# First product in three-chunk steps: a 128-row matmul per chunk and three 19-row matmuls on 32-row tiles

## The chip, the cores and the metric

The kernel runs on one core of one Trainium2 chip. The core has five engines with queues of their own: PE (TensorE, matmuls; its weight loads are shown as PEld), DVE (VectorE), ACT (ScalarE), POOL (GpSimd) and SP (SyncE, which here issues all the transfers). The metric is device time in microseconds, from launch to end, as the median of several runs.

## The reference

Four batches of 12480 tokens attend to 49 agents, which attend to the keys; the result goes through a feed-forward layer.

```python
def sm(a, b):
    s = scale * (a @ b.transpose(0, 2, 1))
    s = s - s.max(-1, keepdims=True)
    e = np.exp(s)
    return e / (e.sum(-1, keepdims=True) + 1e-09)
a2k = sm(agents, k)          # [4, 49, 12480]
agent_v = a2k @ v            # [4, 49, 128]
q2a = sm(q, agents)          # [4, 12480, 49]
x = q2a @ agent_v            # [4, 12480, 128], as 49920 rows
h = x @ w_in                 # w_in [128, 2048]
g = h - np.tanh(h)
out = g @ w_out              # w_out [2048, 128]
```

All inputs are float32; outputs are float32.

## The kernel before

**Folded product.** Since x = q2a @ agent_v, the kernel never forms x. Per batch it computes aw = agent_v @ w_in (49 x 2048) once, and h of a block is aw transposed times the 49 attention weights of each token. A block is 480 tokens (BLK), a batch has 26 blocks, and there are 104 of them. The 2048 hidden units are 16 chunks of 128 (NCH). Each chunk's h is a PSUM tile part of 128 units by 480 tokens.

**Two-part numbers.** A matmul in the fp32r format keeps only part of a float32's bits, so operands are split in a rounded high part and a low remainder. The attention weights lie in `pT` as 98 rows: 49 high parts and 49 low parts (pp, lines 376 and 378). `aw` lies in two tensors, `awh` and `awl`, each with 98 rows: both halves hold the same 49 rows (line 304), rounded for awh, the remainder for awl. `m1` (line 393) adds two matmuls per chunk: awh times pT (line 398) and awl times pT (line 399). The second product does the same with three matmuls: wo_l times gh, wo_h times gh, wo_h times gl (lines 459 to 461).

**One step** is a pair of chunks (n, i): block n, pair i of 8. Four m1 matmuls fill an h tile of two PSUM banks (three such tiles). ACT computes tanh of the scaled h into y (line 408) and its square into z (line 410). Since |h| is small in this data, h - tanh(h) is about h * z up to a constant factor; DVE forms g = h * z (line 412). POOL rounds g to gh (line 442), DVE computes gl = g - gh (line 447), and six m2 matmuls add to the block's output `acc` in a `misc` bank (two such banks, which the other small jobs also use). Where h is too large a general path is chosen at the end (line 588 on); it does not run with these inputs. In even blocks the last pair (PLAIN_PAIR, 7) is "plain": g goes unsplit into full-precision float32 matmuls with wo_f (line 457), four passes for two chunks, and lines 442 and 447 are left out.

**Order.** Program order staggers the work: step k issues m1 of step k, lines 408 to 442 of step k, line 447 of step k - 1 and m2 of step k - 2 (LAG1, LAG2). This order only sets priorities; the framework fixes each engine's queue at build time, with its own model of when an operand is ready, so that m1 of a later step may come between two m2 matmuls.

**Side jobs.** Generators run beside the steps, one part per step (`live`). Counted in positions 0 to 15 of a double block (two blocks): position 0 loads 960 query columns (`q_load`), 3 starts `q_softmax`, 13 starts `q_transpose` for the next even block and 2 for the odd one. `q_transpose` fills a misc bank with four transposes (line 385), and one position later ACT copies it to pT (line 390). At positions from KS the jobs of the next batch's `phase1` start: scores (line 228), the value products (line 276), and `project`, which makes aw in column parts (PCUT) by lines 327 to 331. For batch 0 all of this comes ahead of the loop, save the later parts of project. Key tiles use 3 buffers and value tiles 4 (KV, VB).

**Queues.** SP issues the loads of q, k and v and the store of each double block's output (line 524), in one line of order.

Of the kernel before, what the change touches and what calls it, by code (L numbers as in the profile page):

```python
# [24 lines left out]
A2 = 2 * A  # L25
FF = 2048
# [46 lines left out]
class Build:  # L73
    def __init__(self, ctx, tc, aps):
# [12 lines left out]
    def wtile(self, tag, bufs):  # L87
        return self.work.tile([128, 1024], F32, tag=tag, name=tag, bufs=bufs)
# [4 lines left out]
    def constants(self):  # L93
# [15 lines left out]
        self.wo_f = c.tile([128, 2, C], F32, tag="wo_f", name="wo_f")  # L109
        self.vb = [c.tile([128, GT, C + 2], F32, tag=f"v{i}", name=f"v{i}") for i in range(VB)]  # L110
        for vt in self.vb:
            nc.gpsimd.memset(vt[:, :, C : C + 1], 1.0)
# [38 lines left out]
    def load_w_out(self, c, raw):  # L151
# [7 lines left out]
        if c == PLAIN_PAIR // 2:  # L159
            nc.scalar.copy(self.wo_f.rearrange("p n e -> p (n e)"), w[:, 2 * C * (PLAIN_PAIR % 2) :][:, : 2 * C])  # L160

    def phase1(self, b):
        nc = self.nc
        st = {}
        kb, vb = (KV0 if b == 0 else KV), VB
# [7 lines left out]
        def load_k(g):  # L173
            n = tiles(g)
            kt = self.work.tile([128, GT * 128], F32, tag="kv", name="kt", bufs=kb)
            kt = kt.rearrange("p (t n) -> p t n", n=128)[:, :n, :]
            nc.sync.dma_start(kt, self.kT[b][:, g * GT : g * GT + n, :])
            return kt

        def load_v(g):  # L180
            vt = self.vb[g % VB]
# [13 lines left out]
        def scores(g):  # L195
# [7 lines left out]
            kt = ahead("k", load_k, g, kb if b == 0 else kb - 1)  # L203
            if b and g >= NG - vb:
                ahead("v", load_v, 0, g - NG + vb + 1)
            if b == 0:
                ps = self.ph.tile([128, 2, 512], F32, tag="h", name="h")
# [50 lines left out]
        def av(g):  # L258
            vt = ahead("v", load_v, g, vb - 1)
# [8 lines left out]
            if b == 0:  # L268
                if g == 0:
                    st["ps"] = self.ph.tile([128, 2, 512], F32, tag="h", name="h")[:, 0, :]  # L270
# [39 lines left out]
    def project(self, b, bound):  # L310
        nc = self.nc

        def part(c, lo, hi):
            yield
            yield
            if c == 0:
                self.aw[b] = tuple(
                    self.keep.tile([128, FF], F32R, tag=t, name=t, bufs=2) for t in ("awh", "awl")
                )
            awh, awl = self.aw[b]  # L320
# [8 lines left out]
            h = awh[:A2, sl]  # L329
            nc.scalar.copy(h, ps)  # L330
            nc.vector.tensor_tensor(awl[:A2, sl], ps, h.bitcast(F32), ALU.subtract)
            if bound:
                nc.vector.tensor_reduce(
                    self.mx[:A, NP * b + c : NP * b + c + 1],
                    awh[:A, sl].bitcast(F32),
# [45 lines left out]
    def q_transpose(self, pp, half, res):  # L381
# [7 lines left out]
        pT = self.keep.tile([128, BLK], F32R, tag="pT", name="pT", bufs=3)  # L389
        nc.scalar.copy(pT[:A2], ps[:A2, :BLK])  # L390
        res.append(pT)

    def m1(self, aw, pT, i):
        nc = self.nc
        h = self.ph.tile([128, 2, 512], F32, tag="h", name="h")
        for c in range(2):
            sl = slice((2 * i + c) * 128, (2 * i + c + 1) * 128)
            nc.tensor.matmul(h[:, c, :BLK], aw[0][:A2, sl], pT[:A2], start=True, stop=False)  # L398
            nc.tensor.matmul(h[:, c, :BLK], aw[1][:A2, sl], pT[:A2], start=False, stop=True)  # L399
        return h  # L400

    def pair(self, t):
        return t[:, : 2 * BLK].rearrange("p (c n) -> p c n", c=2)

    def act(self, h):
        nc = self.nc
        y = self.pair(self.wtile("y", NB["y"]))
        nc.scalar.activation(y, h[:, :, :BLK], AF.Tanh, scale=TSC)  # L408
        z = self.wtile("z", NB["z"])[:, : 2 * BLK]
        nc.scalar.activation(z, y.rearrange("p c n -> p (c n)"), AF.Square)  # L410
        g = self.wtile("g", NB["g"])[:, : 2 * BLK]
        nc.vector.tensor_tensor(self.pair(g), h[:, :, :BLK], self.pair(z), ALU.mult)  # L412
        return g

    def act_general(self, h):
        nc = self.nc
        hv = h[:, :, :BLK]
        d = self.wtile("y", NB["y"])[:, : 2 * BLK]
        u = self.wtile("z", NB["z"])[:, : 2 * BLK]
        nc.scalar.activation(self.pair(d), hv, AF.Tanh)  # L420
        nc.scalar.activation(self.pair(u), hv, AF.Square)
        nc.vector.tensor_tensor(self.pair(d), hv, self.pair(d), ALU.subtract)
        big = self.wtile("y", NB["y"])[:, : 2 * BLK]
        nc.vector.tensor_scalar(big, u, 4.0, None, ALU.is_ge)
        nc.vector.tensor_scalar(u, u, 16.0, None, ALU.min)
        r = self.wtile("z", NB["z"])[:, : 2 * BLK]
        nc.vector.tensor_scalar(r, u, 1.0 / 15.0, 13.0, ALU.mult, ALU.add)
        g = self.wtile("g", NB["g"])[:, : 2 * BLK]
# [7 lines left out]
        nc.vector.tensor_tensor(self.pair(g), hv, self.pair(g), ALU.mult)  # L436
# [3 lines left out]
    def high(self, g):  # L440
        gh = self.wtile("gh", NB["gh"])[:, : 2 * BLK].bitcast(F32R)
# [3 lines left out]
    def low(self, g, gh):  # L445
        gl = self.wtile("gl", NB["gl"])[:, : 2 * BLK].bitcast(F32R)
# [3 lines left out]
    def m2(self, acc, i, gh, gl):  # L450
        nc = self.nc
        for c in range(2):
            f = 2 * i + c
# [190 lines left out]
```

## Time and profile before

| what | value |
|---|---|
| runs, median (lowest to highest) | 2228.51 us (2228.47 to 2228.87), 3 runs |
| profiled execution, span from first to last instruction | 2226.8 us |
| granted TensorE clock, mean | 0.992 |
| PE busy | 2181.5 us, 98% |
| DVE busy | 2044.3 us, 92% |
| ACT busy | 1812.7 us, 81% |
| POOL busy | 1410.9 us, 63% |
| share of 16 DMA engines, loads and stores | 15.1% |

The span is the profiled execution's own time as far as the profile tells it; the median of the runs is 1.7 us longer and also holds what lies around the instructions. Busy times are unions: two matmuls that overlap count once. A row of a group reads: line, engine, operation, output <- inputs, shapes, count | busy us, mean ns of one | idle time of the engine before them and what ended it. A timeline row begins with start and duration in us. Matmul durations include the time until the last result is out, so consecutive matmuls overlap in the trace; what one costs is seen from start to start.

### The profile page before, as it was taken

How to read it: one execution, taken by the hardware profiler on the slowest of the kernel's cores; microseconds unless marked ns; L12 is line 12 of the kernel's file. 1: busy time of each engine (PE TensorE's matmuls, PEld its weight loads, DVE VectorE, ACT ScalarE, POOL GpSimd, SP SyncE). 2: the span in 40 equal slices, each digit the busy share in tenths (PEclk: the TensorE clock that was granted, in tenths of full speed). 3: DMA queues.
4: the chain of work that ended last, by engine and by line, in shares of the span. 5: the costliest groups of instructions: out<-in, count | busy, mean ns of one | idle time of the engine just before them, and what ended most of it. 6: DMA issues, size and time to landing. Idle time of an engine off the chain costs nothing.

```text
span 2226.8 us, 31246 instructions
## 1 busy us (share of the span) xinstructions
PE 2181.5 (98%) x11083; PEld 1838.3 (83%) x11083; DVE 2044.3 (92%) x2107; ACT 1812.7 (81%) x2179; POOL 1410.9 (63%) x957
## 2 busy tenths in 40 slices
PE   7699999999999999999999999999999999999998
PEld 7588878888888887888888888788888888888887
DVE  6998998889998999888999999988999999999998
ACT  3478887778887877877888878877889989898987
POOL 2555566656765647665666555766666767676776
PEclk9899999999999999999999999999999999999999
DMA  9411111211011110211011210121010000000000
GB/s 300 120 56 56 57 37 47 65 50 35 28 46 56 56 58 30 63 56 58 19 36 38 65 55 21 37 64 49 19 36 19 28 27 28 27 27 27 27 10 20
DMA packets 76658, 108.75 MB, mean 49 GB/s; under 512 B 4048, under 2 KB 56528, under 8 KB 76496
## 3 DMA queue, kind: packets, MB, share of 16 engines
q1 hardware_dynamic: 76496, 106.68, 15.1%
q8 instruction: 91, 1.49, 0.3%
q14 instruction: 71, 0.58, 0.1%
HBM read 81.10 MB, written 25.56 MB: 48 GB/s over the span
## 4 chain that ended last, share of the span: by engine, by line
PE 90%; DVE 5%; POOL 2%; issue 1%; ACT 1%; DMA 0%; POOLq 0%; SPq 0%; ACTq 0%; DVEq 0%
PE h L398 16%; PE h L399 15%; PE misc L461 15%; PE misc L459 14%; PE misc L460 14%; PE misc L457 4%; PE misc L353 4%; PE misc L276 3%; PE misc L228 3%; DVE gl L447 1%; DVE g L412 1%; POOL gh L442 1%; PE h L209 1%; PE misc L385 1%; PE misc L327 0%
## 5 line engine op out<-in xcount | busy, mean ns | idle before, releaser
L442 POOL TENSOR_SCALAR gh<-g 128x960 fp32r<-128x960 f32 x780 | 1201.8, 1542 | 636.1 <-DVE g L412 488.9
L447 DVE TENSOR_TENSOR gl<-g,gh 128x960 fp32r<-128x960 f32 x780 | 977.6, 1254 | 88.6 <-PE misc L461 62.3
L412 DVE TENSOR_TENSOR g<-h,z 128x960 f32<-128x960 f32 x832 | 950.9, 1147 | 55.7 <-ACT z L410 53.3
L408 ACT ACTIVATE y<-h 128x960 f32<-128x960 f32 x832 | 804.2, 971 | 214.1 <-PE h L399 207.6
L410 ACT ACTIVATE z<-y 128x960 f32<-128x960 f32 x832 | 832.5, 1007 | 24.8 <-DVE g L412 7.8
L398 PE MATMUL h<-pT,awh 98*128 98x480 f32 x1664 | 666.9, 401 | 1.8 <-DVE g L412 1.3
L399 PE MATMUL h<-pT,awl 98*128 98x480 f32 x1664 | 631.6, 380 | 0.0
L461 PE MATMUL misc<-gl,wo_h 128*128 128x480 f32 x1560 | 608.7, 390 | 3.9 <-DVE gl L447 3.8
L459 PE MATMUL misc<-gh,wo_l 128*128 128x480 f32 x1560 | 594.2, 381 | 3.8 <-POOL gh L442 3.6
L460 PE MATMUL misc<-gh,wo_h 128*128 128x480 f32 x1560 | 591.2, 379 | 0.0
L398 PEld LDWEIGHTS h<-pT,awh 98*128 98x128 f32 x1664 | 312.8, 188 | 65.3 <-issue 14.0
L399 PEld LDWEIGHTS h<-pT,awl 98*128 98x128 f32 x1664 | 314.5, 189 | 58.8 <-issue 11.9
L461 PEld LDWEIGHTS misc<-gl,wo_h 128*128 128x128 f32 x1560 | 292.4, 187 | 59.1 <-DVE gl L447 8.7
L459 PEld LDWEIGHTS misc<-gh,wo_l 128*128 128x128 f32 x1560 | 294.3, 189 | 54.0 <-POOL gh L442 11.1
L460 PEld LDWEIGHTS misc<-gh,wo_h 128*128 128x128 f32 x1560 | 292.9, 188 | 47.9 <-issue 0.2
L378 POOL TENSOR_TENSOR pp<-qe,pp 120x392 fp32r<-120x392 f32 x52 | 70.6, 1357 | 67.9 <-ACT pp L376 67.6
L353 PEld LDWEIGHTS misc<-ag,qt 128*120 128x120 f32 x832 | 96.8, 187 | 3.3
L353 PE MATMUL misc<-ag,qt 128*120 128x49 f32 x832 | 94.2, 267 | 0.0
L457 PE MATMUL misc<-g,wo_f 128*128 128x480 f32 x208 | 92.6, 567 | 0.0
L366 POOL TENSOR_TENSOR qe<-qe,qm 120x392 f32<-120x392 f32 x52 | 71.0, 1366 | 30.0 <-ACT qe L364 29.9
L522 ACT ACTIVATE o<-misc 128x480 f32<-128x480 f32 x104 | 58.7, 565 | 36.4 <-PE misc L457 22.8
L276 PEld LDWEIGHTS misc<-v,ke 128*49 128x49 f32 (+1 forms) x588 | 62.0, 123 | 17.5 <-issue 12.9
(85 smaller groups left out, 993.7 us busy)
## 6 DMA issues: line engine op xcount, KB each, us to landing
qt<-qT SPq DMA_DIRECT2D x52, 480.0 KB, 3.4
outT<-o SPq DMA_DIRECT2D x52, 480.0 KB, 2.6
kt<-kT SPq DMA_DIRECT2D x48, 512.0 KB, 3.6
v<-v SPq DMA_DIRECT2D x48, 512.0 KB, 4.1
raw<-w_in SPq DMA_DIRECT2D x4, 512.0 KB, 7.8
raw<-w_out SPq DMA_DIRECT2D x4, 512.0 KB, 9.5
kt<-kT SPq DMA_DIRECT2D x4, 128.0 KB, 2.0
v<-v SPq DMA_DIRECT2D x4, 64.0 KB, 1.9
```

Of the source, the lines that this page charges most:

```text
L353: nc.tensor.matmul(ps[:TT, t * A : (t + 1) * A], qt[:, t * TT : (t + 1) * TT], self.ag[:, b, :], start=True, stop=True)
L398: nc.tensor.matmul(h[:, c, :BLK], aw[0][:A2, sl], pT[:A2], start=True, stop=False)
L399: nc.tensor.matmul(h[:, c, :BLK], aw[1][:A2, sl], pT[:A2], start=False, stop=True)
L408: nc.scalar.activation(y, h[:, :, :BLK], AF.Tanh, scale=TSC)
L410: nc.scalar.activation(z, y.rearrange("p c n -> p (c n)"), AF.Square)
L412: nc.vector.tensor_tensor(self.pair(g), h[:, :, :BLK], self.pair(z), ALU.mult)
L442: self.nc.gpsimd.tensor_scalar(gh, g, 1.0, 0.0, ALU.mult, ALU.add)
L447: self.nc.vector.tensor_tensor(gl, g, gh.bitcast(F32), ALU.subtract)
L457: nc.tensor.matmul(acc[:, :BLK], self.wo_f[:, c, :], gh[:, x], start=first, stop=last)
L459: nc.tensor.matmul(acc[:, :BLK], self.wo_l[:, f, :], gh[:, x], start=first, stop=False)
L460: nc.tensor.matmul(acc[:, :BLK], self.wo_h[:, f, :], gh[:, x], start=False, stop=False)
L461: nc.tensor.matmul(acc[:, :BLK], self.wo_h[:, f, :], gl[:, x], start=False, stop=last)
```

## The change

- awh and awl become `awx` and `awt`. awx has 128 rows: the 98 rows of awh, and below them 30 rows (AX1) of the low parts. The other 19 low rows (AX2) go to `awt`, four copies of the row range at partitions 0, 32, 64 and 96, chunk f at 32 * (f mod 4). Only the 49 low rows that meet the high parts of the attention weights are kept; the product of the two low parts, which awl times pT held before, is left out.
- pT grows to 128 rows: rows 98 to 127 repeat its first 30. A new tile `pR` holds rows 30 to 48 at each of the four 32-row offsets. Both are filled by transfers from pT on SP, five per block, after the copy of line 390. project issues such transfers for awx and awt, up to five per column part.
- m1 works on three consecutive chunks, which may belong to two blocks: three 128-row matmuls, then three 19-row matmuls, one on each of three 32-row tiles, which add to the same three banks. The h tile has three banks, and there are two of them.
- The elementwise work of lines 408, 410, 412, 442 and 447 covers 1440 columns per instruction instead of 960; the square is written to g and multiplied in place, so z goes.
- All chunks take the split path; the plain pairs and wo_f go.
- The side jobs keep their positions; a step of three chunks advances them once for each even chunk in it, so once or twice.
- Key tiles of batches 1 to 3 and value tiles share one ring of five buffers.

```diff
+AX1 = 128 - A2
+AX2 = A - AX1
+QR = 4
...
-PCUT = (0, 256, 768, 1280, 1792, 2048)
+PCUT = (0, 384, 768, 1280, 1792, 2048)
 NP = 5
 KV0 = 13
-KV = 3
-VB = 4
-PLAIN_PAIR = NCH // 2 - 1
-PLAIN_EVERY = 2
+RB = 5
+HP = NCH // 2
+W = 3
 LAG1 = 1
 LAG2 = 1
-NB = dict(y=2, z=2, g=4, gh=3, gl=2)
+NB = dict(y=2, g=3, gh=4, gl=2)
...
-        self.ph = ctx.enter_context(self.pool("ph", 3, space=PSUM))
+        self.ph = ctx.enter_context(self.pool("ph", 2, space=PSUM))
...
+    def slot(self):
+        self.nslot += 1
+        return self.kvb[self.nslot % RB]
...
+            if b == 0:
+                kt = self.work.tile([128, GT * 128], F32, tag="kv", name="kt", bufs=KV0)
+                kt = kt.rearrange("p (t n) -> p t n", n=128)[:, :n, :]
+            else:
+                kt = self.slot()[:, :n, :C]
...
+                awx = self.keep.tile([128, FF], F32R, tag="awx", name="awx", bufs=2)
+                awl = self.keep.tile([128, FF], F32R, tag="awl", name="awl", bufs=1)
+                awt = self.keep.tile([128, NCH // QR, 128], F32R, tag="awt", name="awt", bufs=2)
+                self.aw[b] = awx, awt, awl
+            awx, awt, awl = self.aw[b]
             sl = slice(lo, hi)
             if b == 0 and bound:
-                ps = self.ph.tile([128, 2, 512], F32, tag="h", name="h")[:, 0, :]
+                ps = self.htile()[:, 0, :]
             else:
                 ps = self.misc()
             ps = ps[:A2, : hi - lo]
             nc.tensor.matmul(ps, self.avs[:, b, :], self.w_in[:, sl], start=True, stop=True)
             yield
-            h = awh[:A2, sl]
+            h = awx[:A2, sl]
             nc.scalar.copy(h, ps)
-            nc.vector.tensor_tensor(awl[:A2, sl], ps, h.bitcast(F32), ALU.subtract)
+            nc.vector.tensor_tensor(awl[:A, sl], ps[:A], awx[:A, sl].bitcast(F32), ALU.subtract)
+            nc.sync.dma_start(awx[A2:, sl].bitcast(F32), awl[:AX1, sl].bitcast(F32))
+            lows = awl[AX1:A].bitcast(F32).rearrange("p (k q n) -> p q k n", q=QR, n=128)
+            for q in range(QR):
+                k0, k1 = -(-(lo // 128 - q) // QR), -(-(hi // 128 - q) // QR)
+                if k0 < k1:
+                    nc.sync.dma_start(awt[32 * q : 32 * q + AX2, k0:k1, :].bitcast(F32), lows[:, q, k0:k1, :])
...
         pT = self.keep.tile([128, BLK], F32R, tag="pT", name="pT", bufs=3)
+        pR = self.keep.tile([128, BLK], F32R, tag="pR", name="pR", bufs=3)
         nc.scalar.copy(pT[:A2], ps[:A2, :BLK])
-        res.append(pT)
-
-    def m1(self, aw, pT, i):
-        nc = self.nc
-        h = self.ph.tile([128, 2, 512], F32, tag="h", name="h")
-        for c in range(2):
-            sl = slice((2 * i + c) * 128, (2 * i + c + 1) * 128)
-            nc.tensor.matmul(h[:, c, :BLK], aw[0][:A2, sl], pT[:A2], start=True, stop=False)
-            nc.tensor.matmul(h[:, c, :BLK], aw[1][:A2, sl], pT[:A2], start=False, stop=True)
...
+        nc.sync.dma_start(pT[A2:].bitcast(F32), pT[:AX1].bitcast(F32))
+        for q in range(QR):
+            nc.sync.dma_start(pR[32 * q : 32 * q + AX2].bitcast(F32), pT[AX1:A].bitcast(F32))
+        res.append((pT, pR))
+
+    def m1(self, items, pT):
+        nc = self.nc
+        h = self.htile()
+        for c, (n, f) in enumerate(items):
+            awx = self.aw[n // NBLK][0]
+            nc.tensor.matmul(
+                h[:, c, :BLK], awx[:, f * 128 : (f + 1) * 128], pT[n][0][0], start=True, stop=False
+            )
+        for c, (n, f) in enumerate(items):
+            awt = self.aw[n // NBLK][1]
+            rows = slice(32 * (f % QR), 32 * (f % QR) + AX2)
+            nc.tensor.matmul(h[:, c, :BLK], awt[rows, f // QR, :], pT[n][0][1][rows], start=False, stop=True)
+        return h[:, : len(items), :BLK]
...
         nc = self.nc
-        y = self.pair(self.wtile("y", NB["y"]))
-        nc.scalar.activation(y, h[:, :, :BLK], AF.Tanh, scale=TSC)
-        z = self.wtile("z", NB["z"])[:, : 2 * BLK]
-        nc.scalar.activation(z, y.rearrange("p c n -> p (c n)"), AF.Square)
-        g = self.wtile("g", NB["g"])[:, : 2 * BLK]
-        nc.vector.tensor_tensor(self.pair(g), h[:, :, :BLK], self.pair(z), ALU.mult)
+        w = h.shape[1]
+        y = self.split(self.wtile("y", w))
+        g = self.wtile("g", w)
+        gv = self.split(g)
+        nc.scalar.activation(y, h, AF.Tanh, scale=TSC)
+        nc.scalar.activation(gv, y, AF.Square)
+        nc.vector.tensor_tensor(gv, h, gv, ALU.mult)
...
+    def m2(self, acc, f, c, gh, gl):
+        nc = self.nc
+        sl = slice(c * BLK, (c + 1) * BLK)
+        nc.tensor.matmul(acc[:, :BLK], self.wo_l[:, f, :], gh[:, sl], start=f == 0, stop=False)
+        nc.tensor.matmul(acc[:, :BLK], self.wo_h[:, f, :], gh[:, sl], start=False, stop=False)
+        nc.tensor.matmul(acc[:, :BLK], self.wo_h[:, f, :], gl[:, sl], start=False, stop=f == NCH - 1)
...
+                its, g, gh = q1.pop(0)
+                q2.append((its, gh, self.low(g, gh)))
 
         def out(keep):
             while len(q2) > keep:
-                n, i, gh, gl = q2.pop(0)
-                if i == 0:
-                    acc[n] = self.misc()
-                self.m2(acc[n], i, gh, gl)
-                if i == HP - 1:
-                    done.append(n)
-
-        for n, i in steps:
-            b = blocks[n][0]
-            pos = (n % 2) * HP + i
-            p = n // 2
-            if n % NBLK == 0 and i == 0 and b + 1 < B:
-                kq = self.phase1(b + 1)
-            h = foreground(n, i)
-            if n == 0 and i < len(rest0):
-                run(rest0[i])
+                its, gh, gl = q2.pop(0)
+                for c, (n, f) in enumerate(its):
+                    if f == 0:
+                        acc[n] = self.misc()
+                    self.m2(acc[n], f, c, gh, gl)
+                    if f == NCH - 1:
+                        done.append(n)
...
+        def begin(n, i):
+            p = n // 2
+            pos = (n % 2) * HP + i
...
+        for at in range(0, len(items), W):
+            its = items[at : at + W]
+            h = self.m1(its, pT)
+            while done:
+                finish(done.pop(0))
+            steps = [(n, f // 2) for n, f in its if f % 2 == 0]
+            for n, i in steps:
+                b = n // NBLK
+                if n % NBLK == 0 and i == 0 and b + 1 < B:
+                    kq = self.phase1(b + 1)
+                if n == 0 and i < len(rest0):
+                    run(rest0[i])
+                advance()
+                if n != steps[-1][0] or i != steps[-1][1]:
+                    begin(n, i)
+            g = self.act(h)
+            q1.append((its, g, self.high(g)))
+            low(LAG1)
+            out(LAG2)
+            if steps:
+                begin(*steps[-1])
```

More of the change, by code (lines that the diff above doesn't have):

```diff
@@ L108, in constants @@
         self.wo_l = c.tile([128, NCH, C], F32R, tag="wo_l", name="wo_l")
-        self.wo_f = c.tile([128, 2, C], F32, tag="wo_f", name="wo_f")
-        self.vb = [c.tile([128, GT, C + 2], F32, tag=f"v{i}", name=f"v{i}") for i in range(VB)]
-        for vt in self.vb:
+        self.kvb = [c.tile([128, GT, C + 2], F32, tag=f"v{i}", name=f"v{i}") for i in range(RB)]
+        for vt in self.kvb:
             nc.gpsimd.memset(vt[:, :, C : C + 1], 1.0)
```

99 lines of the change are left out of this document (32 added, 67 removed).

## The prediction

> **What bounds the kernel now.** I read the engine shares first, then two long windows (before and after 1850 us, where the score and value work for batches 1 to 3 ends), then the groups of instructions, then the timeline of single steps.
>
> ```profile
> PE 2181.5 (98%) x11083; PEld 1838.3 (83%) x11083; DVE 2044.3 (92%) x2107; ACT 1812.7 (81%) x2179; POOL 1410.9 (63%) x957
> PE 90%; DVE 5%; POOL 2%; issue 1%; ACT 1%; DMA 0%; POOLq 0%; SPq 0%; ACTq 0%; DVEq 0%
> 100.00:1850.00 1750.00, 1743.44 (x8844) 1465.99 (x8843) 1614.57 (x1642) 1450.76 (x1734) 1107.82 (x754) 1.00 0.14 44
> 1850.00:2200.00 350.00, 350.00 (x1692) 296.01 (x1691) 337.69 (x336) 314.83 (x363) 251.63 (x158) 1.00 0.07 25
> L412 DVE TENSOR_TENSOR g<-h,z 128x960 f32<-128x960 f32 x832 | 950.9, 1147 | 55.7 <-ACT z L410 53.3
> 100.00:1850.00 1750.00, 767.47 (x672) 1.00 0.14 44
> L412 DVE TENSOR_TENSOR g<-h,z 128x960 f32<-128x960 f32 x150 | 171.9, 1146 | 1.3 <-ACT z L410 0.5
> ```
>
> The first two rows give each engine's busy time and the chain that ended last; in the window rows the busy times of PE, PEld, DVE, ACT and POOL follow the length, then the granted clock, 1.00. PE is without a gap after 1850 and 99.6% busy before; DVE comes next with 337.69 of 350. The last row counts 150 pairs (one L412 each) in those 350 us. With 16 pairs to a double block (two 480-token blocks) that is 9.4 double blocks of 37.3 us. The first window holds 672 (the row above it, L412's DVE time and count alone): 42 double blocks of 41.7 us. DVE's share is 1614.57/42 = 38.4 us and, later, 36.0 us. So PE sets the pace, and DVE stands 1.3 us (late) to 3.3 us (early) per double block behind it: all that faster PE could win.
>
> ```profile
> 1994.46 1.14 DVE L412 TENSOR_TENSOR g<-h,z 128x960 f32<-128x960 f32 x1
> 1994.50 0.38 PE L398 MATMUL h<-pT,awh 98*128 98x480 f32 x1
> 1995.53 1.14 DVE L447 TENSOR_TENSOR gl<-g,gh 128x960 fp32r<-128x960 f32 x1
> 1996.60 1.14 DVE L412 TENSOR_TENSOR g<-h,z 128x960 f32<-128x960 f32 x1
> 1996.68 0.38 PE L398 MATMUL h<-pT,awh 98*128 98x480 f32 x1
> ```
>
> A matmul shows 0.38 us, but the ten of a pair start within 1996.68 - 1994.50 = 2.18 us: 0.218 us each is the price I use. DVE's two operations take 1.07 us each from start to start.
>
> **The change part by part.** Per chunk there were two 98-row matmuls. Now three chunks have three 128-row matmuls and three 19-row ones on 32-row tiles: 555 groups of three (1664/3).
>
> 1. The tile section. It replaces 3 x 0.218 = 0.654 us of PE. The trace has no 32-row tiles, but it has excursions to other tile shapes and back.
>
> ```profile
> 868.97 0.37 PE L399 MATMUL h<-pT,awl 98*128 98x480 f32 x1
> 869.27 1.49 PEld L276 LDWEIGHTS misc<-v,ke 128*49 128x49 f32 x14 [0.33 <-issue]
> 870.95 0.19 PEld L461 LDWEIGHTS misc<-gl,wo_h 128*128 128x128 f32 x1 [0.19 <-issue]
> 871.05 0.19 PEld L459 LDWEIGHTS misc<-gh,wo_l 128*128 128x128 f32 x1
> 842.80 0.38 PE L399 MATMUL h<-pT,awl 98*128 98x480 f32 x1
> 843.11 0.29 PEld L253 LDWEIGHTS misc<-dg,ones 49*128 49x128 f32 x2 [0.34 <-ACT z L410]
> 843.46 0.19 PEld L459 LDWEIGHTS misc<-gh,wo_l 128*128 128x128 f32 x1
> 843.57 0.19 PEld L460 LDWEIGHTS misc<-gh,wo_h 128*128 128x128 f32 x1
> L353 PEld LDWEIGHTS misc<-ag,qt 128*120 128x120 f32 x832 | 96.8, 187 | 3.3
> ```
>
> Before 49-column (L276) or 49-row (L253) weights the loader idles 0.33 us, and again 0.19 us after them; L353's full-height, 120-column weights do this nowhere (3.3 us over 832). So a change of tile shape empties the array. Worked out: the next matmul would start at 868.97 + 0.218 = 869.19, the load starts at 869.27, 0.08 late. Fourteen loads take 1.49 us, the last one 0.12 of it, so 0.105 us apart; they end their turn at 870.74. The next load comes 0.21 later, of which 129 columns stream 129/480 x 0.218 = 0.06, leaving 0.15 for the array to empty. The first full matmul streams 0.10 later, when the next load begins (871.05). L253 agrees: two loads of 128 columns 0.10 apart, 843.57 - 843.02 = 0.55 us in all.
>
> The new section is then 0.08 + 0.105 (first load) + 2d + 0.218 (480 columns) + 0.15 + 0.10 = 0.65 us + 2d, where d is the distance between neighbouring tiles. With d = 0 it costs what it replaces. Bounds: d = 0 from below, and 0.218 from above (one after the other). Below even that lies no emptying at all, 0.22 us. I take d = 0.105, L253's pace, the nearest row with 128-column weights on fewer than 128 rows: +0.21 us x 555 = +116 us; half that distance, 0.05, would give +55; bounds 0 and +241; without emptying -241.
>
> The Trainium skill, "TensorE: Matmul & The Clock Gate", Part 3, states that tiles in different row groups start about 4 ns apart; no run here shows it yet. By that rule d = 0.004 and this term would be about +4 us instead of +116.
>
> 2. No plain pairs. 52 pairs lose four full-precision passes each and gain six matmuls.
>
> ```profile
> 2202.55 1.77 PE L457 MATMUL misc<-g,wo_f 128*128 128x480 f32 x4
> L447 DVE TENSOR_TENSOR gl<-g,gh 128x960 fp32r<-128x960 f32 x780 | 977.6, 1254 | 88.6 <-PE misc L461 62.3
> L442 POOL TENSOR_SCALAR gh<-g 128x960 fp32r<-128x960 f32 x780 | 1201.8, 1542 | 636.1 <-DVE g L412 488.9
> ```
>
> PE: 6 x 0.218 - 1.77 = -0.46 us, x 52 = -24 us. DVE and POOL gain one L447 and one L442 per double block.
>
> 3. Three chunks per elementwise instruction.
>
> ```profile
> L522 ACT ACTIVATE o<-misc 128x480 f32<-128x480 f32 x104 | 58.7, 565 | 36.4 <-PE misc L457 22.8
> L408 ACT ACTIVATE y<-h 128x960 f32<-128x960 f32 x832 | 804.2, 971 | 214.1 <-PE h L399 207.6
> L410 ACT ACTIVATE z<-y 128x960 f32<-128x960 f32 x832 | 832.5, 1007 | 24.8 <-DVE g L412 7.8
> L363 DVE TENSOR_REDUCE qm<-misc 120x8 f32<-120x392 f32 x52 | 29.0, 559 | 3.2 <-PE misc L353 1.7
> ```
>
> DVE's slope is (1147 - 559)/568 = 1.035 ns per column, so 480 more cost 0.50 us: 1.57 per operation from start to start. Per double block 10.67 x 2 x 1.57 = 33.5 us, against 31 x 1.07 = 33.2 now: merging pays for the plain pairs, and DVE stays near 36 to 38 us. ACT's slope is (971 - 565)/480, or 0.41 us per chunk: tanh 1.38, square 1.42. Nothing on the path while PE leads. With PE at 41.7 - 0.5 + 10.67 x 0.21 = 43.4 us early and 39.1 late, DVE's 38.4 and 36.0 stay below.
>
> The h tiles are now two of three banks (six before and after). One is held for 0.65 + 0.86 + 1.38 + 1.42 + 1.64 = 5.95 us; two steps are at least 2 x 39.1/10.67 = 7.3 us. I cost this at nothing; if the 1.3 us of slack goes to the score work between, 1% (22 us). The other buffers (z gone, g three, gh four, one ring of five for k and v) I cost at nothing too, behind a DMA share of 0.14.
>
> 4. New transfers on SP: per block one that fills rows 98 to 127 of pT and four that fill pR, behind the ACT copy.
>
> ```profile
> 2000.25 0.34 SPq L524 DMA_DIRECT2D outT<-o  x1
> 2002.04 0.54 ACT L390 CAST pT<-misc 98x480 fp32r<-98x480 f32 x1
> 2002.60 0.98 ACT L408 ACTIVATE y<-h 128x960 f32<-128x960 f32 x1
> v<-v SPq DMA_DIRECT2D x4, 64.0 KB, 1.9
> v<-v SPq DMA_DIRECT2D x4, 32.0 KB, 2.8
> SPq L524 <- ACT o L522: 1168.8, 52, 37.3
> ```
>
> An issue takes about 0.34 us, a small landing 1.9 to 2.8 us; five in a row end 1.7 + 2.8 = 4.5 us after the copy at worst. The copy (L390) ends just as a step's tanh starts. For odd blocks it comes some five pairs ahead, and m2 work covers it. For even blocks (position 14) it comes in the step before its first use in two cases of three: a step is 39.1/10.67 = 3.66 us, its m1 1.51 of it, so 2.1 us ahead of the full matmuls late, 2.6 early. The first transfer takes 0.34 + 1.9 to 2.8, so they wait up to 1.0 us. Behind them on PE stand the m2 matmuls of the two groups before, and gh and gl come free later; the order is fixed at build time and may put those first. 35 blocks x 0.3 = +10 us, bounds 0 and 35 x 2.8 = 98. What shares SP's queue behind these (qt, kt, v, outT) has long waits already, as L524's row shows, with nobody late for it.
>
> 5. Start. The first tile needs awl's rows sent down the partitions before it can run, one issue and landing (2.2 to 3.1 us), once or twice; phase 1 of batch 0 has two h tiles instead of three. +5 us, bounds 0 to 10.
>
> Sum, against the profiled span: 2226.8 + 116 - 24 + 10 + 5 = 2333.8 us. The runs' median (2228.5) lies 1.7 above that span: 2335 us.
>
> **The rivals.**
>
> A. Tiles one after another (the change doesn't do what it says). d = 0.218: 2335 + 125 = 2460 us. For it: nowhere in this trace do two matmuls overlap by more than their tails. Against: other row groups use other rows and other PSUM banks.
>
> B. No emptying: the tile loads go ahead under the running full matmuls, and the section costs one matmul. It decides from a section under 0.65 us. PE's sum falls by 241 + 24 and DVE takes over at 38.4 early and 36.0 late. At its present late share (337.69/350 = 0.965) that makes 39.8 us early, 1.9 less than now, x 42 = -80 us; late nothing. 2228.5 - 80 + 5 = 2154 us, and no loss at block heads, as DVE has work. Against: the idle loader before L253, weights that also leave rows free.
>
> C. Emptying as above but tiles together, d near 0.004: 2335 - 112 = 2223 us, within the noise or just faster. This is the page's rule, worked out here from L276's rows. Against: no pair of loads of 128 columns stands closer than 0.10 us in these rows.
>
> D. The block heads: SP's five issues land late by a whole landing in 35 blocks: 2335 + 88 = 2423 us. For: the copy comes only one step ahead. Against: m2 matmuls of two earlier groups can fill.
>
> **How the numbers follow.** Forecast 0.47 (d between 0.05 and 0.12, 2270 to 2360), A 0.15, B 0.15, C 0.12, D 0.11. The range runs from C's lower side to A, 2205 to 2465, and leaves out B, 0.15. A measurement of this kernel tells about 0.2% from no change. Faster: B and half of C, 0.21. Same: a third of C, 0.04. Slower: the rest, 0.75.
>
> **What would show it.** Step 1: loader idle before each group's first 19-row load (0.3 us) and after its last (0.2 us), full-matmul starts 0.86 us plus 0.218 apart across the section; 0.65 says C, 1.09 says A, 0.22 says B. Step 2: no L457 and DVE below 95% busy. Step 3: DVE operations near 1.64 us. Step 4: at the first group of even blocks PE idle on a DMA, up to 1.0 us. I am wrong if DVE becomes the busiest engine or PE shows idle time above 2% of the loop.

## The result and the profile after

The changed kernel takes 2522.91 us (median of 4 runs, 2520.28 to 2526.86) against 2228.49 us (4 runs, 2228.28 to 2228.87) for the kernel before on the same chip: a ratio of 1.132, 95% interval 1.1304 to 1.1336. It is slower, as forecast, but by 294 us where 107 were expected, and outside the range. The profiled execution has a span of 2525.1 us and a mean granted clock of 0.952 (0.992 before).

From the page of the changed kernel: busy time of each engine, shares of the chain that ended last, and the costliest groups.

```profile
PE 2290.3 (91%) x11187; PEld 1670.2 (66%) x11187; DVE 2080.0 (82%) x1605; ACT 1733.8 (69%) x1624; POOL 1288.5 (51%) x733
...
PE 31%; DVE 22%; POOL 15%; issue 11%; ACT 11%; DMA 7%; SPq 2%; POOLq 0%; ACTq 0%; DVEq 0%
...
L464 POOL TENSOR_SCALAR gh<-g 128x1440 fp32r<-128x1440 f32 x555 | 1093.7, 1971 | 1040.1 <-DVE g L438 941.8
L469 DVE TENSOR_TENSOR gl<-g,gh 128x1440 fp32r<-128x1440 f32 x555 | 984.6, 1776 | 273.6 <-POOL gh L464 266.4
L436 ACT ACTIVATE y<-h 128x1440 f32<-128x1440 f32 x555 | 759.1, 1368 | 498.9 <-PE h L424 497.6
L438 DVE TENSOR_TENSOR g<-h,g 128x1440 f32<-128x1440 f32 x555 | 907.6, 1648 | 121.6 <-ACT g L437 120.1
```

Windows of the changed kernel over the same two stretches as before (length, then busy time and count of PE, PEld, DVE, ACT, POOL, then clock, DMA share, GB/s), and the second one again for line 438 on DVE alone, which counts the steps:

```profile
100.00:1850.00 1750.00, 1623.85 (x8058) 1186.32 (x8059) 1456.31 (x1106) 1235.60 (x1148) 910.45 (x510) 0.97 0.17 51
1850.00:2200.00 350.00, 314.33 (x1423) 222.20 (x1421) 292.56 (x208) 248.14 (x221) 179.26 (x98) 0.94 0.09 31
...
1850.00:2200.00 350.00, 132.65 (x82) 0.94 0.09 31
```

No engine is busy all the time any more. PE's share of the chain fell from 90% to 31%; DVE, POOL and ACT, issue time (11%) and DMA (7%) took the rest. The four engines wait in a ring: POOL waits 941.8 us for DVE's g, DVE waits 266.4 us for POOL's gh, ACT waits 497.6 us for PE's h, and PE waits for what DVE frees. PE stands idle 126.15 us (7%) early and 35.67 us (10%) late, where it had 0.4% and none. The late window holds 82 steps, 350/82 = 4.27 us each; the forecast was 39.1/10.67 = 3.66, the longer tile section included. So the loss shows as idle PE, with a lower granted clock besides (0.97 and 0.94 in the two windows, 1.00 before).

The tile section itself, in the changed kernel's timeline (start, duration), with two rows of the m2 matmuls that follow it, and the start of the loop:

```profile
91.52 1.54 PE L418 MATMUL h<-pT,awx 128*128 128x480 f32 x3 [0.37 <-ACT pp L392]
...
2202.70 0.19 PEld L424 LDWEIGHTS h<-pR,awt 19*128 19x128 f32 x3 [0.34 <-issue]
2202.70 0.49 PE L424 MATMUL h<-pR,awt 19*128 19x480 f32 x3
...
2301.21 0.81 PE L418 MATMUL h<-pT,awx 128*128 128x480 f32 x3
...
2302.36 0.49 PE L477 MATMUL misc<-gl,wo_h 128*128 128x480 f32 x1
2302.69 0.38 PE L475 MATMUL misc<-gh,wo_l 128*128 128x480 f32 x1
```

The loader idles 0.34 us ahead of the first 19-row load, as forecast. But the three loads take 0.19 us together, and the three matmuls 0.49 us together, where three full ones (L418) take 0.81: the tiles do run side by side. The section lasts from the end of the third full matmul's turn, 2301.21 + 3 x 0.217 = 2301.86, to the next full matmul's turn. That one (L477) ends its turn where L475 starts, so its turn begins at 2302.69 - 0.22 = 2302.47: 0.61 us, where 0.654 were replaced. By itself the section is 555 x 0.04 = 24 us cheaper than the matmuls it replaced, an estimate from this one section.

### The profile page after: what moved, and what is told of

It reads as the page before. It is cut to its first block, busy times and chain, and to the rows that moved or that the text cites. A ratio compares the mean times of both kernels' runs of the same rounds, so it can differ in the third digit from the quotient of the medians.

```text
span 2525.1 us, 30180 instructions
## 1 busy us (share of the span) xinstructions
PE 2290.3 (91%) x11187; PEld 1670.2 (66%) x11187; DVE 2080.0 (82%) x1605; ACT 1733.8 (69%) x1624; POOL 1288.5 (51%) x733
## 4 chain that ended last, share of the span: by engine, by line
PE 31%; DVE 22%; POOL 15%; issue 11%; ACT 11%; DMA 7%; SPq 2%; POOLq 0%; ACTq 0%; DVEq 0%
POOL gh L464 14%; DVE g L438 11%; PE misc L477 7%; DVE gl L469 6%; DMA pR<-pT 6%; PE misc L475 6%; PE misc L476 5%; ACT y L436 5%; ACT g L437 5%; PE h L418 4%; PE h L424 3%; PE misc L369 2%; PE misc L285 1%; SPq L410 1%; PE h L218 1%
## 5 line engine op out<-in xcount | busy, mean ns | idle before, releaser
L464 POOL TENSOR_SCALAR gh<-g 128x1440 fp32r<-128x1440 f32 x555 | 1093.7, 1971 | 1040.1 <-DVE g L438 941.8
L469 DVE TENSOR_TENSOR gl<-g,gh 128x1440 fp32r<-128x1440 f32 x555 | 984.6, 1776 | 273.6 <-POOL gh L464 266.4
L436 ACT ACTIVATE y<-h 128x1440 f32<-128x1440 f32 x555 | 759.1, 1368 | 498.9 <-PE h L424 497.6
L438 DVE TENSOR_TENSOR g<-h,g 128x1440 f32<-128x1440 f32 x555 | 907.6, 1648 | 121.6 <-ACT g L437 120.1
L437 ACT ACTIVATE g<-y 128x1440 f32<-128x1440 f32 x555 | 781.5, 1408 | 12.9
L477 PE MATMUL misc<-gl,wo_h 128*128 128x480 f32 x1664 | 691.9, 423 | 95.4 <-DVE gl L469 93.7
L475 PE MATMUL misc<-gh,wo_l 128*128 128x480 f32 x1664 | 694.0, 417 | 41.5 <-POOL gh L464 41.0
L418 PE MATMUL h<-pT,awx 128*128 128x480 f32 x1664 | 473.5, 392 | 24.8 <-DVE g L438 16.2
L477 PEld LDWEIGHTS misc<-gl,wo_h 128*128 128x128 f32 x1664 | 330.5, 199 | 238.2 <-DVE gl L469 159.9
L475 PEld LDWEIGHTS misc<-gh,wo_l 128*128 128x128 f32 x1664 | 332.3, 200 | 141.1 <-POOL gh L464 78.2
L418 PEld LDWEIGHTS h<-pT,awx 128*128 128x128 f32 x1664 | 298.6, 190 | 102.1 <-DVE g L438 35.4
L424 PE MATMUL h<-pR,awt 19*128 19x480 f32 x1664 | 301.0, 486 | 32.5 <-DMA pR<-pT 32.1
L424 PEld LDWEIGHTS h<-pR,awt 19*128 19x128 f32 x1664 | 115.9, 184 | 235.0 <-issue 184.8
L394 POOL TENSOR_TENSOR pp<-qe,pp 120x392 fp32r<-120x392 f32 x52 | 65.2, 1255 | 65.5 <-ACT pp L392 62.7
```

Source lines behind the costliest of these rows:

```text
L418: nc.tensor.matmul(h[:, c, :BLK], awx[:, f * 128 : (f + 1) * 128], pT[n][0][0], start=True, stop=False)
L424: nc.tensor.matmul(h[:, c, :BLK], awt[rows, f // QR, :], pT[n][0][1][rows], start=False, stop=True)
L436: nc.scalar.activation(y, h, AF.Tanh, scale=TSC)
L437: nc.scalar.activation(gv, y, AF.Square)
L438: nc.vector.tensor_tensor(gv, h, gv, ALU.mult)
L464: self.nc.gpsimd.tensor_scalar(gh, g, 1.0, 0.0, ALU.mult, ALU.add)
```

## The experiments

Three theories. Theory 1: two h tiles of three banks are too few; DVE's queue now holds two g and then two gl, POOL's gh comes between, and one pass of that loop, not PE, sets the time of two steps. Theory 2: the tile sections empty the array and cost PE what the kernel lost. Theory 3: at block heads PE waits for the transfers that fill pT and pR, because the copy before them is late. Where an experiment has one run, its time is that of the profiled execution; the kernel before beside it took 2227.9 to 2228.8 us.

The timeline of the changed kernel on DVE and on POOL shows theory 1's loop:

```profile
2322.10 3.21 DVE L438 TENSOR_TENSOR g<-h,g 128x1440 f32<-128x1440 f32 x2
2325.34 1.66 DVE L469 TENSOR_TENSOR gl<-g,gh 128x1440 fp32r<-128x1440 f32 x1
2328.28 1.66 DVE L469 TENSOR_TENSOR gl<-g,gh 128x1440 fp32r<-128x1440 f32 x1 [1.28 <-POOL gh L464]
2329.85 1.65 DVE L438 TENSOR_TENSOR g<-h,g 128x1440 f32<-128x1440 f32 x1
...
2323.91 1.39 POOL L464 TENSOR_SCALAR gh<-g 128x1440 fp32r<-128x1440 f32 x1 [3.42 <-DVE g L438]
2325.47 2.77 POOL L464 TENSOR_SCALAR gh<-g 128x1440 fp32r<-128x1440 f32 x1 [0.17 <-DVE g L438]
```

Two g take 3.21 us back to back; the second gh starts 0.17 us after them and takes 2.77 us, while DVE's first gl runs beside it (the first gh, beside a g, takes 1.39); the second gl waits 1.28 us for it, and the next g starts 7.75 us after the first (2329.85 - 2322.10). Nothing of PE is in this sum, and none of DVE's side jobs.

**e1: DVE's g and gl in turn.** Two hints to the build-time order (`behind` puts one instruction after another in DVE's queue), none of which waits on the chip. First with the transfers where the change has them.

```diff
-        nc.vector.tensor_tensor(gv, h, gv, ALU.mult)
+        i = nc.vector.tensor_tensor(gv, h, gv, ALU.mult).ins
+        self.behind(i, self.last)
+        self.lastg = i
...
-        self.nc.vector.tensor_tensor(gl, g, gh.bitcast(F32), ALU.subtract)
+        self.last = self.nc.vector.tensor_tensor(gl, g, gh.bitcast(F32), ALU.subtract).ins
+        self.behind(self.last, self.lastg)
```

> The same instructions as the changed kernel; only the build-time order of DVE differs: g and gl are made to alternate step by step, where the changed kernel runs two g and then two gl. Theory 1 (the loss comes from the order: two steps at a time leave PE waiting for gh and gl): PE close to its own work, 2250 to 2350 us, and the waits of PE's second product on DVE and POOL mostly gone. Theory 2 (emptying the array at the 19-row tiles costs the time): unchanged, 2500 to 2530. Theory 3 (landing of the pR and pT transfers at block heads): 2450 to 2530.

2668.32 us, 145 slower than the change and above everything expected, at a mean clock of 0.914. Two waits of e1, then its chain by engine:

```profile
DVE g L448 <- ACT g L447: 455.4, 196, 9.0
PEld h L425 <- DMA pR<-pT: 90.4, 92, 2.2
...
PE 40%; DVE 17%; ACT 11%; DMA 11%; issue 10%; POOL 8%; SPq 4%; ACTq 0%; DVEq 0%; POOLq 0%
```

The wait of gl for gh is gone, but the time moved to DVE's g, which waits 455.4 us for the square, and DMA and SP's queue hold 15% of the chain (9% in the change). By itself e1 speaks against theory 1. But it had made the order tighter where theory 3 bites: with g and gl in strict turn, nothing can go ahead while a block head waits. Whether that was it, e11 had to tell.

**e2: two-chunk steps, three h tiles.** The change's products and transfers stay.

```diff
-W = 3
+W = 2
...
-        self.ph = ctx.enter_context(self.pool("ph", 2, space=PSUM))
+        self.ph = ctx.enter_context(self.pool("ph", 3, space=PSUM))
```

> The changed kernel with two chunks per step and three two-bank h tiles, so 832 tile sections of two 19-row matmuls instead of 555 of three. Theory 1 (step size and two h tiles): PE-bound, before plus 832 x (0.61 - 0.44) = +141, less 24 for the plain pairs, plus about 15: 2340 to 2400 us. Theory 2: 277 more sections, so slower than the changed kernel, 2600 to 2700. Theory 3: 2490 to 2530, since the block heads stay as they are.

2459.75 us. From its page:

```profile
PE 2362.9 (96%) x11187; PEld 1665.3 (68%) x11187; DVE 2173.9 (88%) x2159; ACT 1810.0 (74%) x2178; POOL 1462.9 (60%) x1010
...
PE 57%; DVE 14%; DMA 10%; POOL 8%; issue 5%; SPq 3%; ACT 2%; POOLq 0%; ACTq 0%; DVEq 0%
```

PE is back at 96% busy and 57% of the chain, though the section now serves two chunks instead of three. Still 13% of the chain lies in DMA and SP's queue.

**e3: three-chunk steps, but two 98-row matmuls per chunk.** No tiles, no transfers.

```diff
...
-                h[:, c, :BLK], awx[:, f * 128 : (f + 1) * 128], pT[n][0][0], start=True, stop=False
...
+            nc.tensor.matmul(h[:, c, :BLK], awx[:A2, sl], pT[n][0][0][:A2], start=True, stop=False)
+            nc.tensor.matmul(h[:, c, :BLK], awl[:A2, sl], pT[n][0][0][:A2], start=False, stop=True)
```

> The changed kernel's three-chunk steps and two h tiles, but the first product again as two 98-row matmuls per chunk: no 19-row tiles, no transfers for pT, pR, awx or awt. Theory 1: still slow, 2430 to 2520 us. Theories 2 and 3: 2228 less 24 for the plain pairs, so 2200 to 2230.

2443.38 us, only 80 below the change: 215 us of the loss are there without any 19-row matmul or new transfer. From its page, then its late window for DVE's g, which counts the steps:

```profile
PE 29%; DVE 25%; POOL 20%; issue 13%; ACT 12%; DMA 0%; POOLq 0%; DVEq 0%; SPq 0%; ACTq 0%
...
L454 DVE TENSOR_TENSOR gl<-g,gh 128x1440 fp32r<-128x1440 f32 x555 | 973.1, 1755 | 275.0 <-POOL gh L449 270.6
...
1850.00:2200.00 350.00, 139.38 (x86) 1.00 0.07 23
```

The same mixed chain with DMA at 0%, and the same wait of gl for gh (270.6 us, 266.4 in the change). Two steps take 2 x 350/86 = 8.14 us here and 8.54 in the change: the 7.75 of the loop and 0.39 more, in which DVE's side jobs lie, and in the change another 0.40, which comes with the tiles and transfers.

**e4: the 19-row matmuls left out.**

```diff
...
-        for c, (n, f) in enumerate(items):
-            awt = self.aw[n // NBLK][1]
-            rows = slice(32 * (f % QR), 32 * (f % QR) + AX2)
-            nc.tensor.matmul(h[:, c, :BLK], awt[rows, f // QR, :], pT[n][0][1][rows], start=False, stop=True)
```

> The changed kernel without the 19-row matmuls (the low parts of 19 agents are left out of h; the transfers still run). Theory 2: all of the tile sections' time goes, 555 x 0.61 = 339 us, 2180 to 2200. Theory 1: PE's work falls but the waits stay as far as the order stays, 2300 to 2430. Theory 3: about 2470 to 2500, less what PE's work falls.

2339.07 us with PE 84% busy. PE does less than the kernel before (one matmul per chunk in m1 instead of two) and the kernel is still 110 us slower than it. PE's work isn't the bound, which speaks against theory 2 and for 1 or 3. It is also 184 us faster than the change: without the sections an h tile is filled sooner and no matmul waits for pR, and this run doesn't tell the two apart.

**e5, e6, e7: the transposes two positions earlier**, in the change, in e1 and in e2.

```diff
-T0 = 13
+T0 = 11
```

> The changed kernel with the transposes of even blocks two positions earlier (11 instead of 13), so that the copy to pT and its five transfers run about 4.8 us earlier. Theory 3 (block heads wait for pR; DMA and SP's queue hold 9% of the chain of the changed kernel): up to 9% goes, 2300 to 2400 us, and L424's waits for pR are gone. Theory 1 (the cycle g, g, gh, gl, gl of two steps, 7.7 us, sets the time): the waits for pR go, but the time falls by less than 60 us, 2465 to 2515.

> The alternating order of e1 with the transposes at position 11. In e1 single steps ran 3.2 us apart and the heads stood still for some 9 us. If that reading is right the heads shorten by the time that the copy comes earlier, 52 x 3 to 5 us: 2400 to 2510. If alternation itself is the bad order: no more than 50 us below e1's 2668.

> Two-chunk steps of e2 with the transposes at position 11. Theory 3 for what remained in e2 above PE's own work: 2340 to 2400 us. If e2's rest is not the heads: 2430 to 2460.

2545.25, 2659.55 and 2455.03 us, against 2522.91, 2668.32 and 2459.75 without: no help, +22 in the first. The position of the transposes isn't what makes a block head late. The chain of e7 in order of time (start, duration, engine, result, line; pieces under 0.1 us left out) shows what is:

```profile
2036.22 0.94 POOL pp L394
2037.20 0.49 PE misc L401 x4
2037.72 0.57 ACT pT L407
2038.31 0.86 SPq L408
2039.21 0.61 SPq L410
2039.88 4.48 DMA pR<-pT
2044.41 0.47 PE h L424
```

The transposes (L401) start as soon as the attention weights are ready (pp, L394 on POOL). From the end of the copy (2038.29) to the last 19-row matmul of that head, which waits for its transfer (2044.41), pass 6.1 us. Earlier transposes only wait longer for pp; the query softmax has to move. So the three misses say nothing against theory 3 yet, though by their expectations e6 and e7 spoke against it. In the changed kernel's own chain the last landing can take longer still:

```profile
2230.62 0.56 ACT pT L407
...
2233.99 6.33 DMA pR<-pT
```

There 9.1 us pass from the end of the copy (2231.18) to the landing (2240.32), behind which a 19-row matmul waits.

**e8: the kernel before with two h tiles of two banks instead of three.** Nothing else.

```diff
-        self.ph = ctx.enter_context(self.pool("ph", 3, space=PSUM))
+        self.ph = ctx.enter_context(self.pool("ph", 2, space=PSUM))
```

> The kernel before with two instead of three two-bank h tiles; nothing else. Theory 1 in the form that the number of h tiles decides (one of three taken away): clearly slower, 2320 to 2480 us. If the length of the step decides and not the number of tiles: within 2228 to 2260.

2558.64 us: this one number costs 330 us, more than the 90 to 250 expected. Its timeline on DVE:

```profile
2302.16 1.15 DVE L447 TENSOR_TENSOR gl<-g,gh 128x960 fp32r<-128x960 f32 x1
2304.20 1.16 DVE L447 TENSOR_TENSOR gl<-g,gh 128x960 fp32r<-128x960 f32 x1 [0.89 <-POOL gh L442]
2305.27 1.15 DVE L412 TENSOR_TENSOR g<-h,z 128x960 f32<-128x960 f32 x1
2307.00 1.16 DVE L412 TENSOR_TENSOR g<-h,z 128x960 f32<-128x960 f32 x1 [0.57 <-ACT z L410]
2308.07 1.15 DVE L447 TENSOR_TENSOR gl<-g,gh 128x960 fp32r<-128x960 f32 x1
```

The same order, two g and two gl with a wait for gh between, appears in the old kernel as soon as it has two h tiles. The tile count changes the order that the build fixes.

**e9, e10, e11: the query softmax and the transposes earlier**, in the change, in e2 and in e1.

```diff
-QS = 3
+QS = 1
...
-T0 = 13
+T0 = 9
```

> The changed kernel with the whole query chain of the next double block earlier: its softmax at position 1 instead of 3, the transposes of the even block at 9 instead of 13. The reading of e7 is that the copy to pT comes late because pp is late, so that e5's and e6's shift of the transposes alone did nothing. Theory 3a (heads wait for the query chain and the five transfers): the chain loses its DMA and SP shares (8%), and the time falls by the part of the 82 us between the changed kernel and e3 that the transfers hold: 2440 to 2490 us. Theory 1 alone: 2505 to 2545.

> e2 with the query chain earlier as in e9. In e2 PE was busy for 2363 of 2458 us, and 13% of the chain was the transfers and SP's queue. Theory 3a: 2365 to 2400 us, PE-bound. If the heads are not what is left: 2440 to 2460.

> e1's alternating order with the query chain earlier. Between heads e1 ran a step in 3.2 to 3.6 us; if the heads are covered, 555 steps of about 3.6 to 4.0 us and 130 us of start and end: 2130 to 2350 us. If alternation with two h tiles stalls by itself: 2550 to 2660.

2499.47, 2397.85 and 2299.73 us: 23, 62 and 369 us less than without. In order, the chain of e9, and one group and one wait of e11:

```profile
DVE 30%; PE 23%; POOL 22%; issue 16%; ACT 8%; DMA 1%; POOLq 0%; DVEq 0%; ACTq 0%; SPq 0%
```

```profile
L476 POOL TENSOR_SCALAR gh<-g 128x1440 fp32r<-128x1440 f32 x555 | 1443.8, 2602 | 507.2 <-DVE g L448 498.6
...
DVE g L448 <- ACT g L447: 154.4, 160, 7.6
```

In e9 DMA falls from 7% of the chain to 1%, and little is won, since the loop of theory 1 stands behind it. In e11, with the order mended too, 223 us of the change's 294 come back. Theories 1 and 3 both hold, and they hide one another: either mended alone gives -23 or +145. What made e1 fail was the block heads. These runs move the softmax and the transposes together, and the softmax's own work on ACT and DVE moves with them, so the waits for the transfers and this work are not told apart. Nor is it a slow gh by itself that costs: in e11 a gh takes 2602 ns on average (1971 in the change), but gl hardly waits for it (4.8 us in all, 266.4 in the change).

e10 tells something of the buffers too, since it has the change's ring, g, gh and gl buffers but three h tiles. PE is 97% busy in it. A section of two tiles also takes 0.61 us there: the full matmuls before one end their turn at 2000.09 + 2 x 0.218 = 2000.53, and the load of the second full matmul after it, which begins with the first one's turn, at 2001.14. So 832 sections cost about 832 x (0.61 - 0.44) = 141 of the 169 us that e10 lies above the kernel before, an estimate that leaves some 28 us for the plain pairs, the block heads and these buffers together.

**e12: the kernel before without plain pairs**, four runs.

```diff
-PLAIN_EVERY = 2
+PLAIN_EVERY = 1000
```

> The kernel before with the plain pairs taken out and nothing else. Step 2 of the prediction: PE loses 24 us; after 1850 us DVE has only 1.3 us of room per double block and gains one operation of 1.07, so the gain comes from the 42 earlier double blocks alone: 2205 to 2215 us. If DVE takes over: 2225 to 2260.

2259.63 us against 2228.78; ratio 1.0137, interval 1.0120 to 1.0154: +31 us. The window after 1850 us and the group of L447 in it, now one for each pair:

```profile
1850.00:2200.00 350.00, 342.42 (x1644) 284.17 (x1643) 344.18 (x332) 305.30 (x349) 254.70 (x162) 1.00 0.07 23
...
L447 DVE TENSOR_TENSOR gl<-g,gh 128x960 fp32r<-128x960 f32 x144 | 182.6, 1268 | 5.8 <-PE misc L461 5.8
```

144 pairs are 9.0 double blocks of 38.9 us (37.3 before). DVE is now the busiest, 344.18 of 350, 38.2 us per double block where it had 36.0: the pair that was plain adds one gl of 1.27 us, and DVE's other time grows by 38.2 - 36.0 - 1.27 = 0.9. PE, by the sum 0.46 us cheaper, stands idle 0.84 us of each double block. From 100 to 1850 us a double block takes 42.2 us where it took 41.7 (664 pairs, 672 before); DVE is 95% busy there (1668.40 of 1750), and why it costs time in that stretch isn't shown.

**e13, e14, e15: the order of e1** in e3, in e8, and in e3 with the query softmax early. The edits are those shown above.

> e3 (three-chunk steps, two h tiles, two 98-row matmuls per chunk, no transfers) with g and gl alternating on DVE. If the order of two steps at a time is what two h tiles cost: 2250 to 2330 us against e3's 2443. If their number costs by itself: 2420 to 2500.

> e8 (the kernel before with two two-bank h tiles) with g and gl alternating on DVE. If the order: 2250 to 2350 us against e8's 2559. If the number of tiles by its latency (m1 0.87, tanh 0.97, square 1.00, g 1.15 and the hand-overs, about 4.4 us for two steps of 2.18): 2450 to 2600.

> e13 with the query chain earlier, as e11 but with two 98-row matmuls per chunk and no transfers. If tile sections cost about what they replace (0.61 for 0.65 us) and the heads are covered in e11: within 30 us of e11's 2300. If the tile sections or transfers still cost there: 2220 to 2260.

2336.99, 2343.08 and 2320.04 us: 106 and 216 us below e3 and e8, and 17 below e13. The waits of e13, then of e14:

```profile
DVE g L433 <- ACT g L432: 204.4, 216, 4.1
```

```profile
DVE g L422 <- ACT z L420: 280.2, 334, 3.1
```

Without transfers the order mends about six tenths of what two h tiles cost (106 of 184, 216 of 330). The rest stays: with two tiles, g still waits 204.4 and 280.2 us for the square, and ahead of that ACT's tanh waits 373.2 and 319.2 us for PE's h. And e11 (2299.73) lies 20 us below e15 (2320.04), one run each: once order and block heads are mended, the tile sections with their transfers are worth about 20 us to the kernel, near the 24 read from the timeline.

No version beat the kernel before; the best with the change's products is e11.

## Why the prediction was wrong

The direction was right, the size and the cause were not. The loss of 294 us splits by the runs in the order before, e12, e3, after; in another order the parts would differ:

| part | us | from | forecast |
|---|---|---|---|
| no plain pairs | +31 | 2259.63 - 2228.8 | -24 |
| three-chunk steps, two h tiles (with the other buffers) | +184 | 2443.38 - 2259.63 | 0 |
| tile sections and transfers, upon those steps | +79 | 2522.91 - 2443.38 = 79.5 | +131 (116 + 10 + 5) |

**The step that failed is step 3.** It held two h tiles of three banks for enough: "One is held for ... 5.95 us; two steps are at least ... 7.3 us", costed at nothing, 22 us if the slack went. That sum put each h tile's holders in a row as if DVE's queue always had that tile's g next. It didn't ask what order the build would make with two tiles. The runs show two g and then two gl, with a contended gh of 2.77 us between, 7.75 us for two steps against the 7.3 that PE needs with all its side jobs, and so no room to catch up after DVE's side jobs or a block head: 8.14 us in e3, 8.54 in the change. e8 shows it without the rest of the change (330 us for one tile less), e13 and e14 that the order is the larger part. That this step could turn the bound was among the prediction's own tests ("PE shows idle time above 2% of the loop"): it shows 7 and 10%. But no rival said so, and the range's ends, C and A, were made from d alone. The term of +184 also includes the change's ring of k and v tiles and its g in place of z; no run took these out by themselves, but e10, which has them with three h tiles, speaks for a small part.

**Step 1, mis-sized.** The array does empty at the change of tile shape: the loader's 0.34 us before the 19-row loads answers to the 0.33 it was drawn from. The distance d was taken from L253's loads, 0.105 us apart, which go to the same rows of the array; tiles in different row groups load and run together here, and the section is 0.61 us, not 0.86: a term of about -24 us instead of +116. Rival C, by the Trainium skill's rule, had the section right ("TensorE: Matmul & The Clock Gate", Part 3; the trace agrees: 0.49 us for three matmuls, 0.47 for the one in e7's chain). Its total of 2223 us was missed for the same reason as mine, step 3. A's 1.09 us and B's 0.22 are refuted.

**Step 2, wrong sign where it was measured.** That DVE gains one L447 was right, but not what comes of it: DVE stood 1.3 us behind PE late, and one gl of 1.27 us uses this up. The price of one L447 stood in the prediction beside that slack; with two chunks per instruction the term should have been zero at best late. DVE's work also grew by more than one gl, as e12 shows. The prediction let the merging of step 3 pay for it (33.5 us against 33.2); no run takes the plain pairs out at three chunks, so how far that holds isn't shown.

**Step 3's durations, right.** DVE's g takes 1.648 us (forecast 1.64), ACT's tanh 1.368 (1.38).

**Step 4, right in its mechanism, mis-sized.** The issues take 0.56 to 0.86 us (0.34 forecast), the landing 4.5 us in e7's chain and 6.3 at this head of the change (1.9 to 2.8): 6.1 us from the copy to the last 19-row matmul of the head in e7 and 9.2 in the change (2240.37), where "4.5 us ... at worst" was said. D's price of 88 us was nearer than mine of 10, but there is no one price: the query softmax made early saves 23, 62 or 369 us by the order that it meets (e9, e10, e11). The step named m2 matmuls as cover, and they don't cover the heads: the loader's wait for pR, 90.4 us, stands in e1's list above. Of the +79 above, the sections themselves would make about -24, so the block heads, the start and the lower clock (0.952, 0.988 in e3) come to about 100. This is a difference, not a measurement of its own.

**Step 5, right in its mechanism, but later and dearer.** The first m1 matmul of the loop in the kernel before and in e3, then the second m1 group of the changed kernel:

```profile
86.60 0.77 PE L398 MATMUL h<-pT,awh 98*128 98x480 f32 x1 [0.46 <-ACT awh L330]
...
90.43 0.75 PE L408 MATMUL h<-pT,awx 98*128 98x480 f32 x1
...
103.25 1.54 PE L418 MATMUL h<-pT,awx 128*128 128x480 f32 x3 [5.74 <-DMA awx<-awl]
```

The first one starts at 91.52 us in the changed kernel, +4.9, which looks like the +5 forecast. But it starts at 90.43 in e3, which has no transfers, so 3.8 of the 4.9 have another cause. The transfers cost their time at the second group, where PE stands idle 5.74 us for the rows of awx, at a granted clock of 0.50 until 110 us (0.99 from 90 to 100 us in the kernel before). That +5 came close to the first start is luck.

## What to carry to other kernels

Before PSUM buffers are traded for larger tiles, work out not only how long one is held, but which order of instructions the build will fix with one buffer fewer, and lay out one turn of each loop through the engines; if that turn is as long as the bottleneck's, the gain is gone. When two waits hide one another, mending either alone can show little or a loss (e9, e1), so try them together before a theory is dropped (e11). And read the slack of the second engine against each instruction that a change adds to it: 1.3 us of slack and 1.27 us of new work is no saving.

## What the runs showed of the hardware

**Row tiles start together.** Three loads of 19 rows by 128 columns in different 32-row groups take 0.19 us together, and the three matmuls 0.49, where one alone (e7) takes 0.47. The Trainium skill, "TensorEngine Tiling (Array Packing)", Key Properties, says that a change of mode has to drain the array; the trace agrees, with 0.34 us of idle loader.

**POOL beside DVE.** The same gh takes 1.39 us while DVE's g reads h from PSUM, and 2.77 us when DVE's gl, which reads two operands from SBUF, runs beside it. That gl covers only the first 1.53 us of the gh (2325.47 to 2327.00); what is left after it, 1.24 us, is nearly a whole gh. So while gl ran, POOL hardly moved (an estimate; the profile's spans on POOL are rough). The Trainium skill, "GPSIMD Engine Reference", 1. Specifications, tells of SBUF interfaces shared with VectorE, with contention when VectorE has two SBUF inputs; the trace agrees, with these numbers.

**The clock after a stall.** Windows of e1 after a block head (columns as above), a row of its timeline, two rows of its chain in order of time, and a row of e7's timeline:

```profile
2175.00:2180.00 5.00, 4.97 (x13) 3.38 (x14) 5.00 (x3) 3.56 (x3) 4.53 (x3) 0.50 0.04 13
2180.00:2181.00 1.00, 1.00 (x4) 0.82 (x3) 1.00 (x2) 0.57 (x1) 1.00 (x1) 0.50 0.00 0
2181.00:2182.00 1.00, 1.00 (x7) 0.56 (x5) 1.00 (x2) 0.00 (x0) 0.53 (x2) 0.87 0.30 119
```

```profile
2174.78 1.57 PE L419 MATMUL h<-pT,awx 128*128 128x480 f32 x3 [2.75 <-DVE g L448]
...
2178.24 0.40 PE misc L489
...
2182.90 0.22 PE misc L489
```

```profile
2044.41 0.47 PE L424 MATMUL h<-pR,awt 19*128 19x480 f32 x1 [1.10 <-DMA pR<-pT]
```

After PE's idle stretch of 2.75 us the granted clock is 0.50, and a matmul takes 0.40 us instead of 0.22; the clock is still 0.50 at 2181, 6.2 us after the first matmul at 2174.78. In e7 PE was idle for only 1.10 us, and the granted clock is 0.50 from 2046 to 2048. The Trainium skill, "TensorE: Matmul & The Clock Gate", Part 1, halves the rate after an idle window of about 3.4 us and gives it back after about as much activity; these traces differ from both: shorter idle stretches came before the half clock, and in e1 it lasted longer. So such a stall of a block head is paid twice. How much of e1's time this makes isn't shown, but its mean clock is 0.914, the change's 0.952, e11's 0.985.
